# Ten token blocks with split products, loads moved behind the streamed sums, and plain last steps in a fused attention and rational expert kernel

## The chip, the cores and the metric

The kernel runs on one core of one Trainium2 chip. The metric is the device time of one execution in microseconds (us). The kernel before took 936.82 us (median of 2 runs, 936.0 to 937.63). The execution that the profiler recorded took 939.04 us; its span, from the first to the last instruction in the trace, is 937.3 us.

## The reference

Attention within chunks of 64 tokens (8 batches, 8 heads, 576 tokens, head size 64), and on its output a two-layer product with a rational function between:

```python
scores = scale * np.matmul(q_c, k_c.transpose(0, 1, 2, 4, 3))
attn = np.exp(scores - np.max(scores, axis=-1, keepdims=True))
attn = attn / (np.sum(attn, axis=-1, keepdims=True) + 1e-09)
x = np.matmul(attn, v_c)            # reshaped to 4608 tokens x 512
h = x @ w_in                        # 512 -> 2048
P = a[0] + a[1] * h + a[2] * h2 + a[3] * h3
Q = 1.0 + np.abs(b[0]) * np.abs(h) + np.abs(b[1]) * h2
g = P / (Q + 1e-06)
out = g @ w_out                     # 2048 -> 512
```

All inputs and the output are 32-bit floats.

## The kernel before

The 4608 tokens are cut into 18 blocks of 256 (`NB`), and the 2048 middle columns into 4 steps of 512 (`NST`), so there are 72 steps, numbered g = 4 x block + step. 32-bit values are kept as a high part and a low part, and a product of two such values is three matmuls: high by high, low by high, high by low.

**First layer.** A step's `ph` (512 middle columns by 256 tokens, a pair of PSUM banks) is 48 matmuls of 128x256 at L347 (`ff1`, in two halves that the order calls `F` and `Fb`). The first of them in a step multiplies `xhi` by `wi_hi`, the last multiplies `xhi` by `wi_lo`.

**The rational function.** ScalarE makes `U` = |h| and `C` from `ph`; VectorE and ScalarE work in turn until VectorE's third `C` instruction at L486 leaves g in `C` (entry `g` of the order).

**Second layer.** Up to block 5 a step is plain: ScalarE casts g to `ghi` (L496), GpSimd makes `glo` (L540), and TensorE does 48 matmuls at L423 into `po`. From block 6 on (`fast`) the product is a scheme of seven products of half the size each way: `graw` holds three quarters of g as they are, `shi`/`slo` four sums and differences of quarters (`B`, made on GpSimd at L505 to L537), and TensorE does 18 matmuls on `graw` (entries `Zr`, `Zr2`) and 24 on `shi` and `slo` (`Zs`, `Zl`), 42 in place of 48, at L594 into `acc` and `acd`. Four of the seven products need sums of quarters of w_out. They were made once, on GpSimd, during blocks 3 to 5 (`making`: up to six operations behind each `lS`; tiles `tt` and `hh`), and sent to scratch memory `t` (L568), 2 MB for each of the four steps. They don't all fit on the chip, so each step fetches its own from `t` again (`fetch`, L579): two transfers of 256 KB once `Zr2` has used the old ones (slot 0), one of 768 KB behind `Zs` and one behind `Zl` (slots 1 to 3). The sum products of the next step read them.

**Queue.** All transfers go through the queue of SyncE (SP): these fetches, `v` of the next block (L130, 512 KB, issued where the attention has used the old v, entry `A`), `qT` and `kT` of the next block (L754, 512 KB each, issued behind the scores, entry `S`), and the four stores of a block's output (L640, 128 KB each). An issue that has to wait, because its buffer is still read, holds up the ones behind it.

**Order.** In the steady state the string `STEADY` sets the order, entry by entry for a block; `_2` is a step, `-1` and `+1` the block before and after. Attention of the next block is spread over the entries in capitals with `+1`. Before it a hand-made list (`START`) covers 12 steps. TensorE runs a step's `ph` (48), then 42 products of the second layer of two steps back, and so on.

**End.** Behind the last `ph` come the second layer of the last two steps, then one copy (L624) and four additions (L630 to L636) that join `acc` and `acd` to the output tile `o`, and four stores.

Of the kernel before, what the change touches and what calls it, by code (L numbers as in the profile page):

```python
# [50 lines left out]
STEADY = (  # L51
# [6 lines left out]
)  # L58
# [6 lines left out]
def tile_chunked_attention_rational_moe(  # L65
# [28 lines left out]
    cst = cp.tile([P, 2], F32, tag="cst", name="cst")  # L94
    co = cp.tile([P, 32], F32, tag="co", name="co")
    a0, a1, a2, a3 = (ab[:, i:i + 1] for i in range(4))
# [3 lines left out]

    na0, na1, na2, na3, c0, kq, lsc, ebias, ib, b1m, nib = (co[:, i:i + 1] for i in range(11))
    TINY = 2.0 ** -60
# [228 lines left out]


    ch, gbuf, obuf, accs = {}, {}, {}, {}
# [94 lines left out]
    def newton_coefficients():  # L428
# [9 lines left out]
        ts(ebias, ebias, -KLN * math.log(2.0), None, ALU.add)  # L438

    def fast(g):  # L440
        return steps[g][0] >= FAST

# [88 lines left out]
    def new_ls(g):  # L531
# [3 lines left out]
        if fast(g):  # L535
            lo = gbuf[key][1] = p2.tile([P, 4, 2, 128], F32R, tag="glo", name=f"slo{g}")
            nc.gpsimd.tensor_sub(lo, sbuf[g], hi.bitcast(F32))  # L537
        else:
            lo = gbuf[key][1] = p2.tile([P, FPS, BT], F32R, tag="glo", name=f"glo{g}")
            nc.gpsimd.tensor_sub(lo, C, hi.bitcast(F32))  # L540

# [6 lines left out]
    def sums_of(s, tt, hh):  # L548
        def whole(dst, k, half):
            nc.gpsimd.tensor_add(dst, w_part(0, k, s, half).bitcast(F32), w_part(1, k, s, half).bitcast(F32))  # L550

        T = [tt[:, i] for i in range(4)]
        yield lambda: whole(T[1], 0, 0)
        yield lambda: whole(T[3], 0, 1)
        yield lambda: nc.gpsimd.tensor_sub(T[1], T[3], T[1])
        yield lambda: whole(T[2], 1, 1)
        yield lambda: nc.gpsimd.tensor_add(T[3], T[2], T[3])
        yield lambda: nc.gpsimd.tensor_add(T[2], T[2], T[1])
        yield lambda: whole(T[0], 1, 0)
        yield lambda: nc.gpsimd.tensor_sub(T[0], T[0], T[2])  # L560

        def low(i):
            nc.gpsimd.tensor_sub(tt[:, i], tt[:, i], hh[:, i].bitcast(F32))

        def send():
            scratch[s] = dr.tile([P, 2, 4, 512], F32, tag=f"t{s}", name=f"t{s}")
            nc.sync.dma_start(out=scratch[s][:, 0], in_=hh.bitcast(F32))
            nc.sync.dma_start(out=scratch[s][:, 1], in_=tt)  # L568

        yield lambda: nc.scalar.copy(hh[:, 1:4:2], tt[:, 1:4:2])  # L570
# [15 lines left out]

    def fast_product(n, s, name, j, stat, h, start, stop):
        where = FAST_B[name]
# [3 lines left out]
        else:  # L592
            mov = wo[:, h, FPS * where[3] + 2 * j, 256:512]
        nc.tensor.matmul(acc[n][pair][:, bank, col:col + 256], stat, mov, start=start, stop=stop)  # L594

# [3 lines left out]
    def fast_raw(g, half):  # L599
# [3 lines left out]
        for name in "124":  # L603
            for j in range(2):
                for h in ((0, 1) if half == 0 else (0,)):
                    stat = graw[g % 2][:, half, j, RAW[name]]
                    fast_product(n, s, name, j, stat, h, s == 0 and half == 0 and j == 0 and h == 0, False)

    def fast_sum(g, half):
        n, s = steps[g]  # L610
        for name in "5673":
            for j in range(2):
                for h in ((0, 1) if half == 0 else (0,)):
                    stat = gbuf[n, s][half][:, SUM[name], j]
                    fast_product(
                        n, s, name, j, stat, h, s == 0 and half == 0 and j == 0 and h == 0 and name == "7",
                        s == NST - 1 and half == 1 and j == 1,
                    )

    def fast_out(n, k):  # L620
# [14 lines left out]
        else:  # L635
            add(o[:, 1], one_[:, 1, 0:256], o[:, 1])  # L636
            for c in range(2):
                for u in range(UPB):
                    half = o[64 * u:64 * u + 64, 2 - 2 * c:4 - 2 * c].rearrange("p a b -> p (a b)")
                    (nc.scalar if n == NB - 1 and u else nc.sync).dma_start(out=rows_out(n)[c, u], in_=half)  # L640

# [87 lines left out]

    total = len(steps)  # L730
# [4 lines left out]
    making = [f for s in range(NST) for f in sums_of(s, tt, hh)]  # L735

# [12 lines left out]
    def next_scores(n):  # L749
        att_s(n, tag=other())  # L750
        if n + 1 < NB:
            for i, (src, key) in enumerate(((qT, "q"), (kT, "k"))):
                loaded[key, n + 1] = qk[:, i, :]
                nc.sync.dma_start(out=qk[:, i, :], in_=src[n + 1])  # L754

    def values(n):
        att_av(n, tag=other())
        load_v(n + 1)

# [6 lines left out]
    def step_op(op, g):  # L766
# [6 lines left out]
        elif op in chain:  # L773
            chain[op](g)
            if op == "lS":
                for _ in range(6):
                    if making:
                        making.pop(0)()
        elif not fast(g):
# [3 lines left out]
            elif op == "Zl":  # L783
                ff2(n, s, "po", 2)
                if n == FAST - 1:
                    for h in range(2):
                        fetch(0, slice(s, s + 1), h)
        elif op in ("Zr", "Zr2"):
            fast_raw(g, op == "Zr2")
            if op == "Zr2" and g + 1 < total:  # L790
                for h in range(2):
                    fetch((s + 1) % NST, slice(0, 1), h)
        else:
            fast_sum(g, op == "Zl")
            if g + 1 < total:
                fetch((s + 1) % NST, slice(1, 4), 1 if op == "Zs" else 0)

    items = [re.fullmatch(r"(\w+?)(?:_(\d))?([+-]\d+)?", item).groups() for item in STEADY.split()]
    for b in range(FIRST // NST, NB + 1):
        for op, stage, shift in items:  # L800
            n = b + int(shift or 0)
# [6 lines left out]
            elif op in ("P1", "o1", "o2", "o3", "o4"):  # L808
                if n >= FAST:
                    fast_out(n, ("P1", "o1", "o2", "o3", "o4").index(op))  # L810
                elif op == "P1" and n not in made["O"]:
                    store(n)
# [38 lines left out]
```

## Time and profile before

| | |
|---|---|
| time, median of 2 runs | 936.82 us |
| the profiled execution | 939.04 us, span 937.3 us |
| TensorE (PE) busy | 870.3 us, 93% of the span, 9096 matmuls |
| VectorE (DVE) busy | 749.6 us, 80% |
| ScalarE (ACT) busy | 562.9 us, 60% |
| GpSimd (POOL) busy | 506.2 us, 54% |
| DMA | 164.93 MB, mean 176 GB/s |
| mean granted TensorE clock | 0.978 |

The shares are means over the whole span: the first 280 us (loading, preparing the weights, the plain steps) look different from the 620 us behind them, in which blocks follow each other in about 48 us. The end, some 35 us without new `ph`, differs again. A view of waits says for how long an engine stood because something else was late, and what came last; a view of windows says the same by stretch. The chain of waits follows the end of the program backwards.

### The profile page before, as it was taken

What the parts mean: (1) busy time and instruction counts of PE and PEld (TensorE: products, weight loads), DVE (VectorE), ACT (ScalarE), POOL (GpSimd) and SP (SyncE); (2) the same over time, 40 slices, a digit from 0 to 9 for tenths busy, and PEclk for the clock granted to TensorE, in tenths of its full rate; (3) what the DMA queues carried; (4) which work ended last, traced back from release to release, by engine and by line L of the source; (5) the groups of instructions that cost most, each with busy time, mean ns of one, the idle gap of its engine ahead of it and who ended that gap; (6) DMA issues with size and microseconds to landing.
All of it is one profiled execution on the core that took longest, in us unless ns stands there. A gap on an engine that the chain in (4) does not pass through costs nothing.

```text
span 937.3 us, 20950 instructions
## 1 busy us (share of the span) xinstructions
PE 870.3 (93%) x9096; PEld 848.7 (91%) x9096; DVE 749.6 (80%) x673; ACT 562.9 (60%) x602; POOL 506.2 (54%) x318
## 2 busy tenths in 40 slices
PE   2799999989989999998999999999989999999985
PEld 1789999989989999898998999998989999999985
DVE  6899999867767687887778797878878889897771
ACT  4799966464455655555465656556556565666550
POOL 0114210236668635666567666675756767676672
PEclk9799999999999999999999999999999999999997
DMA  7455422102233243767576766667667777666673
GB/s 290 159 181 172 155 80 77 38 21 66 96 135 136 70 165 100 232 212 237 180 247 204 229 212 218 221 208 232 206 195 226 226 222 224 210 210 197 206 232 112
DMA packets 119099, 164.93 MB, mean 176 GB/s; under 512 B 5856, under 2 KB 104160, under 8 KB 115936
## 3 DMA queue, kind: packets, MB, share of 16 engines
q1 hardware_dynamic: 118848, 163.34, 54.4%
q8 instruction: 71, 1.16, 0.5%
q10 hardware_dynamic: 160, 0.26, 0.1%
q14 instruction: 20, 0.16, 0.1%
HBM read 145.76 MB, written 17.83 MB: 175 GB/s over the span
## 4 chain that ended last, share of the span: by engine, by line
PE 72%; DMA 13%; ACT 6%; DVE 5%; POOL 3%; issue 1%; DVEq 0%; SPq 0%; POOLq 0%; ACTq 0%
PE ph L347 34%; PE acc L594 12%; DMA wo<-t 11%; PE acd L594 10%; PE po L423 10%; PE psx L220 2%; DMA raw<-in_w_in 2%; PE pst L299 2%; PE pss L220 2%; ACT at L303 1%; DVE sm L256 1%; POOL glo L540 1%; DMA t<-tt 1%; POOL tt L550 1%; DVE e L262 1%
## 5 line engine op out<-in xcount | busy, mean ns | idle before, releaser
L347 PE MATMUL ph<-xhi,wi_hi 128*128 128x256 f32 x1152 | 326.1, 283 | 10.8 <-ACT at L303 6.4
L347 PE MATMUL ph<-xlo,wi_hi 128*128 128x256 f32 x1152 | 322.5, 280 | 0.1
L347 PE MATMUL ph<-xhi,wi_lo 128*128 128x256 f32 x1152 | 322.3, 280 | 0.0
L347 PEld LDWEIGHTS ph<-xhi,wi_hi 128*128 128x128 f32 x1152 | 217.8, 189 | 16.2 <-ACT at L303 8.6
L347 PEld LDWEIGHTS ph<-xlo,wi_hi 128*128 128x128 f32 x1152 | 217.8, 189 | 0.5 <-DVE xlo L330 0.4
L347 PEld LDWEIGHTS ph<-xhi,wi_lo 128*128 128x128 f32 x1152 | 217.9, 189 | 0.0
L537 POOL TENSOR_TENSOR slo<-B,shi 128x1024 fp32r<-128x1024 f32 x48 | 121.7, 2536 | 85.3 <-ACT shi L529 85.3
L478 DVE SCALAR_TENSOR_TENSOR U<-U,co,ph 128x1024 f32<-128x1024 f32 x60 | 75.7, 1261 | 58.2 <-ACT ph L474 58.2
L457 DVE SCALAR_TENSOR_TENSOR U<-U,co 128x1024 f32<-128x1024 f32 x60 | 98.9, 1649 | 26.4 <-ACT U L448 26.4
L448 ACT ACTIVATE U<-ph 128x1024 f32<-128x1024 f32 x60 | 61.5, 1025 | 91.4 <-PE ph L347 91.4
L505 POOL TENSOR_TENSOR graw<-C,graw 128x768 fp32r<-128x768 f32 x48 | 98.7, 2055 | 31.0 <-ACT graw L500 24.6
L513 POOL TENSOR_TENSOR B<-C 128x512 f32<-128x512 f32 x48 | 75.1, 1564 | 70.7 <-DVE C L486 70.7
L470 ACT ACTIVATE B<-U,cst,co 128x1024 f32<-128x1024 f32 x60 | 74.8, 1246 | 54.7 <-DVE U L457 54.7
L461 DVE TENSOR_TENSOR C<-C,ph 128x1024 f32<-128x1024 f32 x60 | 72.8, 1214 | 33.6 <-ACT U L448 33.6
L423 PE MATMUL po<-wo,ghi 128*128 128x256 f32 (+2 forms) x768 | 93.5, 278 | 0.0
L453 ACT ACTIVATE C<-ph,co 128x1024 f32<-128x1024 f32 x60 | 72.2, 1204 | 31.2 <-PE ph L347 28.0
L423 PEld LDWEIGHTS po<-wo,ghi 128*128 128x128 f32 x768 | 90.6, 188 | 0.0
L594 PE MATMUL acc<-wo,graw 128*128 128x256 f32 x576 | 84.6, 281 | 1.5 <-POOL graw L505 1.5
L474 ACT ACTIVATE ph<-B,co 128x1024 f32<-128x1024 f32 x60 | 67.2, 1120 | 29.1 <-DVE C L465 26.8
L594 PE MATMUL acd<-wo,shi 128*128 128x256 f32 x384 | 64.5, 292 | 21.6 <-DMA wo<-t 19.9
L486 DVE SCALAR_TENSOR_TENSOR C<-C,co,ph 128x1024 f32<-128x1024 f32 x60 | 76.9, 1281 | 2.1
L465 DVE SCALAR_TENSOR_TENSOR C<-C,co,ph 128x1024 f32<-128x1024 f32 x60 | 76.6, 1276 | 1.1
(107 smaller groups left out, 1630.8 us busy)
## 6 DMA issues: line engine op xcount, KB each, us to landing
wo<-t SPq DMA_DIRECT2D x94, 768.0 KB, 6.5
wo<-t SPq DMA_DIRECT2D x102, 256.0 KB, 3.5
v<-in_vP SPq DMA_DIRECT2D x18, 512.0 KB, 4.8
out<-o SPq DMA_DIRECT2D x70, 128.0 KB, 2.6
raw<-in_w_in SPq DMA_DIRECT2D x8, 1024.0 KB, 4.8
raw<-in_w_out SPq DMA_DIRECT2D x8, 1024.0 KB, 4.8
qk<-in_qT SPq DMA_DIRECT2D x16, 512.0 KB, 3.6
qk<-in_kT SPq DMA_DIRECT2D x16, 512.0 KB, 5.0
```

Of the source, the lines that this page charges most:

```text
L347: nc.tensor.matmul(ph[:, fi, :], w[:, cc, f], x[:, cc, :], start=(k == 0), stop=(k == len(mm) - 1))
L423: nc.tensor.matmul(accs[n][i][:, cols], g[:, fi, i * 128:(i + 1) * 128], w[:, FPS * s + fi, cols], start=start, stop=stop,)
L457: nc.vector.scalar_tensor_tensor(U, U, c0, U, ALU.add, ALU.mult)
L461: nc.vector.tensor_mul(C, C, h)
L465: nc.vector.scalar_tensor_tensor(C, C, na1, h, ALU.add, ALU.mult)
L470: nc.scalar.activation(ch[key][2], ch[key][1], AF.Ln, bias=cst[:, 0:1], scale=lsc)
L478: nc.vector.scalar_tensor_tensor(V, V, kq, h, ALU.add, ALU.mult)
L486: nc.vector.scalar_tensor_tensor(C, C, na0, h, ALU.add, ALU.mult)
L505: nc.gpsimd.tensor_sub(lo, quads(ch[steps[g]][3])[:, :, 1:4, :], hi.bitcast(F32))
L513: nc.gpsimd.tensor_sub(S[:, 0:2], q[:, 0:1].to_broadcast([P, 2, 2, 128]), q[:, 1:3])
L537: nc.gpsimd.tensor_sub(lo, sbuf[g], hi.bitcast(F32))
L594: nc.tensor.matmul(acc[n][pair][:, bank, col:col + 256], stat, mov, start=start, stop=stop)
```

## The change

Six things change together.

1. **Parts.** In blocks 7 to 16 certain matmuls are written as two, each for a part of the 256 columns of the moving operand, with the same stationary operand. F is the first `ph` product of a step, f the last, r the first product on `graw`, l the last on `slo`. The cuts are 152/104 (MOST), 128/128 (EVEN) and 208/48 (SOME). Twelve products by four steps are cut, 48 more matmuls in all.
2. **Loads.** `qk`, `v` and the output stores no longer go out at their own entries. They are put on a list, and behind each step's last fetch two entries of the list are sent: `qT`/`kT` in four pieces of 256 columns (128 KB each), `v` in two halves of 256 KB, the stores in pairs. Two entries are 512 KB.
3. **Last steps.** `fast` leaves out g = 70 and 71. They are plain steps again, 96 matmuls in place of 84, into a bank pair of their own (`pe`); `glo` is made on VectorE. The quarters of w_out that the fetches overwrite are kept in scratch `b` and loaded again as `b12` (1 MB, at the start of the last block). The joining of `acc` and `acd` is done before, and two additions into `oe` and stores of 256 KB (halves on two queues) end the program.
4. **Making.** `making` is cut into groups: four operations, four operations, then copies, low parts and the send, so that twelve `lS` entries carry it and no longer ten.
5. **Order.** `STEADY` has another order of entries for VectorE, ScalarE and GpSimd. TensorE's order of entries is the same.
6. **Places.** The tile of constants `co` moves to another pool, and `graw` starts 384 bytes into its buffer.

```diff
+    PARTS = {
+        7: {"F": MOST}, 8: {"r": MOST}, 9: {"F": MOST, "r": MOST}, 10: {"F": EVEN}, 11: {"r": EVEN},
+        12: {"f": MOST}, 13: {"l": MOST}, 14: {"f": MOST, "l": MOST}, 15: {"F": SOME}, 16: {"r": SOME},
+    }
...
             for k, (w, x, cc) in enumerate(mm):
-                nc.tensor.matmul(ph[:, fi, :], w[:, cc, f], x[:, cc, :], start=(k == 0), stop=(k == len(mm) - 1))
+                at_ = "F" if fi == 0 and k == 0 else "f" if fi == FPS - 1 and k == len(mm) - 1 else ""
+                cuts = parts_of(n, at_)
+                for i, (a_, b_) in enumerate(cuts):
+                    nc.tensor.matmul(
+                        ph[:, fi, a_:b_], w[:, cc, f], x[:, cc, a_:b_], start=(k == 0 and i == 0),
+                        stop=(k == len(mm) - 1 and i == len(cuts) - 1),
+                    )
...
     def fast(g):
-        return steps[g][0] >= FAST
+        return NST * FAST <= g < total - 2
...
-            graw[g % 2] = p2.tile([P, 2, 2, 3, 128], F32R, tag="raw", name=f"graw{g % 2}", bufs=3)
+            t = p2.tile([P, 96 + 1536], F32R, tag="raw", name=f"graw{g % 2}", bufs=3)
+            graw[g % 2] = t[:, 96:].rearrange("p (h j q t) -> p h j q t", h=2, j=2, q=3)
...
+    def tail_load():
+        b12 = p2.tile([P, 2, 2, 2, 256], F32R, tag="raw", name="b12", bufs=3)
+        tail["b12"] = b12
+        for k in range(2):
+            nc.sync.dma_start(out=b12.bitcast(F32)[:, k], in_=scratch["b", 2 + k])
...
-                nc.sync.dma_start(out=qk[:, i, :], in_=src[n + 1])
+            for c in range(4):
+                def send(c=c):
+                    cols = slice(256 * c, 256 * c + 256)
+                    for i, src in enumerate((qT, kT)):
+                        nc.sync.dma_start(out=qk[:, i, cols], in_=src[n + 1][:, cols])
+
+                later.append(send)
...
-                for _ in range(6):
-                    if making:
-                        making.pop(0)()
+                while making:
+                    f = making.pop(0)
+                    if f is None:
+                        break
+                    f()
...
+        elif g == total - 2:
+            if op in ("Zr", "Zl"):
+                tail_next(int(op == "Zl"))
+        elif g == total - 1:
+            if op == "Zl":
+                tail_last()
...
             fast_sum(g, op == "Zl")
-            if g + 1 < total:
+            if fast(g + 1):
                 fetch((s + 1) % NST, slice(1, 4), 1 if op == "Zs" else 0)
+            if op == "Zl":
+                later_loads()
+
+    def later_loads():
+        for f in later[:2]:
+            f()
+        del later[:2]
...
+        if b == NB - 1:
+            tail_load()
```

The queue of SP, one block in the steady state, before. `t` is a step's scratch, `wo` the place that the products read.

```order
L640 DMA out<-o_6278 64x512 x4
L579 DMA wo<-t_2883 128x2x256 x2
L130 DMA v_6407<-in_vP 128x1024
L579 DMA wo<-t_2883 128x6x256 x2
L754 DMA qk<-in_qT 128x1024
L754 DMA qk<-in_kT 128x1024
L579 DMA wo<-t_3179 128x2x256 x2
L579 DMA wo<-t_3179 128x6x256 x2
L579 DMA wo<-t_3631 128x2x256 x2
L579 DMA wo<-t_3631 128x6x256 x2
```

The same stretch of SP's queue in the changed kernel:

```order
L721 DMA out<-o_6933 64x512 x4
L604 DMA wo<-t_3471 128x2x256 x2
L604 DMA wo<-t_3471 128x6x256 x2
L852 DMA v_7060<-in_vP 128x512 x2
L604 DMA wo<-t_3931 128x2x256 x2
L604 DMA wo<-t_3931 128x6x256 x2
L842 DMA qk<-in_qT 128x256
L842 DMA qk<-in_kT 128x256
```

Before, one step's fetches have 1 MB of `qk` ahead of them and the slots 1 to 3 of another have `v`; now each step's fetches come first, and 512 KB of other transfers follow them.

GpSimd while the sums of w_out are made, before:

```order
L550 TENSOR_TENSOR tt<-wo 128x512 x2
L555 TENSOR_TENSOR tt<-tt 128x512
L550 TENSOR_TENSOR tt<-wo 128x512
L557 TENSOR_TENSOR tt<-tt 128x512
L558 TENSOR_TENSOR tt<-tt 128x512
L540 TENSOR_TENSOR glo_2454<-C_2200,ghi_2399 128x1024
L550 TENSOR_TENSOR tt<-wo 128x512
L560 TENSOR_TENSOR tt<-tt 128x512
L563 TENSOR_TENSOR tt<-tt,hh 128x512 x2
L540 TENSOR_TENSOR glo_2584<-C_2338,ghi_2535 128x1024
L563 TENSOR_TENSOR tt<-tt,hh 128x512 x2
L550 TENSOR_TENSOR tt<-wo 128x512 x2
```

and in the changed kernel:

```order
L557 TENSOR_TENSOR glo_2452<-C_2197,ghi_2377 128x1024
L576 TENSOR_TENSOR tt<-tt 128x512
L577 TENSOR_TENSOR tt<-tt 128x512
L567 TENSOR_TENSOR tt<-wo 128x512
L579 TENSOR_TENSOR tt<-tt 128x512
L557 TENSOR_TENSOR glo_2611<-C_2336,ghi_2494 128x1024
L583 TENSOR_TENSOR tt<-tt,hh 128x512 x4
L557 TENSOR_TENSOR glo_2744<-C_2530,ghi_2661 128x1024
L567 TENSOR_TENSOR tt<-wo 128x512 x2
```

Before, the first operations of the next step's sums (L550, which overwrite `tt`) stand directly behind the last operations of this step's, with only the transfer that empties `tt` between; now a `glo` stands there.

The end of VectorE's program, before (the last rational function, then the joining of `acc` and `acd`):

```order
L461 TENSOR_TENSOR C_10437<-C_10437,ph_3_10366 128x1024
...
L478 SCALAR_TENSOR_TENSOR U_10439<-U_10439,co,ph_3_10366 128x1024
L482 SCALAR_TENSOR_TENSOR ph_3_10366<-U_10439,ph_3_10366 128x1024
L486 SCALAR_TENSOR_TENSOR C_10437<-C_10437,co,ph_3_10366 128x1024
L630 TENSOR_TENSOR o_10590<-acc_10305,o_10590 128x2x256
L632 TENSOR_TENSOR o_10590<-acd_10306,o_10590 128x2x256
L634 TENSOR_TENSOR o_10590<-acd_10306,o_10590 128x512
L636 TENSOR_TENSOR o_10590<-acc_10305,o_10590 128x256
```

and in the changed kernel:

```order
L494 SCALAR_TENSOR_TENSOR U_10579<-U_10579,co,ph_3_10509 128x1024
L557 TENSOR_TENSOR glo_10622<-C_10460,ghi_10581 128x1024
L498 SCALAR_TENSOR_TENSOR ph_3_10509<-U_10579,ph_3_10509 128x1024
L502 SCALAR_TENSOR_TENSOR C_10584<-C_10584,co,ph_3_10509 128x1024
L557 TENSOR_TENSOR glo_10677<-C_10584,ghi_10659 128x1024
L708 TENSOR_TENSOR o_10679<-acc_10443,o_10679 128x2x256
...
L714 TENSOR_TENSOR o_10679<-acc_10443,o_10679 128x256
L692 TENSOR_TENSOR oe_10709<-pe,o_10679 128x512
L692 TENSOR_TENSOR oe_10737<-pe,o_10679 128x512
```

The two `glo` of the last steps have come to VectorE, and the four additions stand ahead of the last two, which alone read the last products (`pe`).

## Rows read from the trace of the kernel before

**Rows 1.** The profile's page, section 2: in 40 equal slices of the span the granted clock of TensorE in tenths of full speed, and the busy share of the DMA engines in tenths.

```profile
PEclk9799999999999999999999999999999999999997
DMA  7455422102233243767576766667667777666673
```

**Rows 2.** What TensorE waited for over the whole span: the waiting operation and its line, what came last, then us in total, times, and the longest.

```profile
PE acd L594 <- DMA wo<-t: 20.5, 12, 3.7
...
PE ph L347 <- ACT at L303: 6.4, 11, 4.7
```

**Rows 3.** The same view for 367 to 902 us alone, in which the seven-product steps follow each other.

```profile
PE acd L594 <- DMA wo<-t: 14.6, 9, 3.0
```

**Rows 4.** Busy time by windows, each one block of the steady state, and the sum over nine such windows: the window, its length, busy us of the engines (and instructions), granted clock, DMA share, GB/s.

```profile
433.23:484.31 51.08, 47.97 (x497) 47.08 (x497) 40.01 (x36) 28.16 (x28) 31.53 (x21) 0.97 0.66 207
484.31:532.27 47.96, 45.72 (x497) 44.86 (x497) 39.65 (x36) 28.15 (x28) 31.83 (x21) 1.00 0.70 222
...
726.57:773.49 46.92, 46.38 (x497) 45.32 (x497) 39.61 (x36) 28.18 (x28) 32.17 (x21) 1.00 0.72 224
...
sum 435.45, PE 417.58 PEld 409.48 DVE 360.48 ACT 253.41 POOL 287.01; mean PE 46.40 PEld 45.50 DVE 40.05 ACT 28.16 POOL 31.89
```

**Rows 5.** The chain of waits from 484 to 535 us: start, us, what.

```profile
484.18 10.07 DMA wo<-t
...
495.08 0.45 PE acc L594 x4
...
497.34 5.44 PE ph L347 x48
502.79 0.94 PE acc L594 x8
...
504.67 0.70 PE acd L594 x6
...
508.72 5.92 PE ph L347 x48
```

**Rows 6.** The timeline of SP's queue from 460 to 505 us: start, us until the end of the piece, line, transfer, number.

```profile
480.81 0.35 SPq L754 DMA_DIRECT2D qk<-in_qT  x1
...
481.74 23.56 SPq L579 DMA_DIRECT2D wo<-t  x9
```

**Rows 7.** The fetches issued between 484.1 and 485 us: time from issue to landing.

```profile
DMA to landing us min/median/max: 10.1/10.1/10.1
```

**Rows 8.** The two fetches issued between 496 and 498 us, in a step without other transfers: when, and time from issue to landing.

```profile
L579 SPq DMA_DIRECT2D wo<-t x2: 359/360/360, 496.0 to 497.1; - x2
...
DMA to landing us min/median/max: 4.7/5.3/5.8
```

**Rows 9.** The page's section 6, issues of transfers: number, KB each, median us from issue to landing.

```profile
wo<-t SPq DMA_DIRECT2D x94, 768.0 KB, 6.5
...
out<-o SPq DMA_DIRECT2D x70, 128.0 KB, 2.6
...
qk<-in_kT SPq DMA_DIRECT2D x16, 512.0 KB, 5.0
```

**Rows 10.** Busy time by short windows: two right behind the two longest waits of the steady state, and one without a wait before it (columns as in rows 4).

```profile
444.00:448.60 4.60, 4.41 (x24) 4.44 (x25) 4.50 (x7) 2.51 (x3) 3.44 (x4) 0.63 0.26 71
686.30:690.80 4.50, 4.35 (x24) 4.38 (x25) 4.40 (x6) 2.42 (x3) 3.82 (x4) 0.62 0.37 107
590.00:592.90 2.90, 2.72 (x23) 2.75 (x24) 2.86 (x3) 1.65 (x2) 2.82 (x3) 1.00 0.51 165
```

**Rows 11.** The chain of waits while the sums of w_out are made, 225 to 275 us.

```profile
229.25 2.38 POOL glo L540
...
235.14 6.76 DMA t<-tt
...
260.87 7.36 PE ph L347 x48
```

**Rows 12.** The timeline of VectorE at the end of the program: start, us, line, operation.

```profile
912.81 1.28 DVE L486 SCALAR_TENSOR_TENSOR C<-C,co,ph 128x1024 f32<-128x1024 f32 x1
...
932.00 0.69 DVE L634 TENSOR_TENSOR o<-acd,o 128x512 f32<-128x512 f32 x1
932.60 0.41 DVE L636 TENSOR_TENSOR o<-acc,o 128x256 f32<-128x256 f32 x1
```

**Rows 13.** The chain of waits at the end of the program.

```profile
902.98 0.94 PE acc L594 x8
...
907.72 6.53 DMA wo<-t
...
919.45 5.93 DMA wo<-t
```

**Rows 14.** Busy time by windows at the end of the program (columns as in rows 4).

```profile
907.93:930.11 22.18, 14.72 (x84) 13.76 (x83) 4.76 (x4) 4.12 (x4) 10.66 (x7) 0.77 0.54 175
```

**Rows 15.** The casts to `ghi` on ScalarE, a group by line: number, busy us, mean ns of one, idle before.

```profile
L496 ACT CAST ghi<-C 128x1024 fp32r<-128x1024 f32 x12 | 12.5, 1044 | 2.9 <-DVE C L486 2.9
```

**Rows 16.** Products of the plain second layer (L423), shapes apart: number, busy us, mean ns of one, idle before.

```profile
L423 PE MATMUL po<-wo,ghi 128*128 128x304 f32 x32 | 9.5, 297 | 0.0
L423 PE MATMUL po<-wo,ghi 128*128 128x208 f32 x32 | 8.3, 259 | 0.0
```

More of the change, by code (lines that the diff above doesn't have):

```diff
@@ L568, in send @@
             nc.sync.dma_start(out=scratch[s][:, 1], in_=tt)
+            if s >= 2:
+                scratch["b", s] = dr.tile([P, 2, 2, 256], F32, tag=f"b{s}", name=f"b{s}")
+                rows = slice(FPS * s, FPS * s + 3, 2)
+                for h in range(2):
+                    nc.sync.dma_start(out=scratch["b", s][:, h], in_=wo.bitcast(F32)[:, h, rows, 256:512])
         yield lambda: nc.scalar.copy(hh[:, 1:4:2], tt[:, 1:4:2])
@@ L593, in fast_product @@
             mov = wo[:, h, FPS * where[3] + 2 * j, 256:512]
-        nc.tensor.matmul(acc[n][pair][:, bank, col:col + 256], stat, mov, start=start, stop=stop)
+        cuts = parts_of(n, place_)
+        for i, (a_, b_) in enumerate(cuts):
+            nc.tensor.matmul(
+                acc[n][pair][:, bank, col + a_:col + b_], stat, mov[:, a_:b_],
+                start=start and i == 0, stop=stop and i == len(cuts) - 1,
+            )
     RAW = {"1": 0, "2": 2, "4": 1}
@@ L606, in fast_raw @@
                     stat = graw[g % 2][:, half, j, RAW[name]]
-                    fast_product(n, s, name, j, stat, h, s == 0 and half == 0 and j == 0 and h == 0, False)
+                    first = s == 0 and half == 0 and j == 0 and h == 0
+                    at_ = "r" if half == 0 and j == 0 and h == 0 and name == "1" else ""
+                    fast_product(n, s, name, j, stat, h, first, False, at_)
     def fast_sum(g, half):
@@ L636, in fast_out @@
             add(o[:, 1], one_[:, 1, 0:256], o[:, 1])
+            if n == NB - 1:
+                return
             for c in range(2):
-                for u in range(UPB):
-                    half = o[64 * u:64 * u + 64, 2 - 2 * c:4 - 2 * c].rearrange("p a b -> p (a b)")
-                    (nc.scalar if n == NB - 1 and u else nc.sync).dma_start(out=rows_out(n)[c, u], in_=half)
+                def send(c=c):
+                    for u in range(UPB):
+                        half = o[64 * u:64 * u + 64, 2 - 2 * c:4 - 2 * c].rearrange("p a b -> p (a b)")
+                        nc.sync.dma_start(out=rows_out(n)[c, u], in_=half)
+                later.insert(c, send)
     def rows_out(n):
@@ L727, in tile_chunked_attention_rational_moe @@
     run(START, "F")
-    total = len(steps)
+    co = p2.tile([P, 32], F32, tag="co", name="co", bufs=1)
+    na0, na1, na2, na3, c0, kq, lsc, ebias, ib, b1m, nib = (co[:, i:i + 1] for i in range(11))
     newton_coefficients()
@@ L734, in tile_chunked_attention_rational_moe @@
     qk = p2.tile([P, 2, W], F32, tag="raw", name="qk", bufs=3)
-    making = [f for s in range(NST) for f in sums_of(s, tt, hh)]
+    making = [f for s in range(NST) for f in sums_of(s, tt, hh)][1:]
     made = {name: {int(args.split(".")[0]) for name_, args, _ in START_ITEMS if name_ == name} for name in "SEZTKAXYNO"}
@@ L753, in next_scores, with send @@
                 loaded[key, n + 1] = qk[:, i, :]
-                nc.sync.dma_start(out=qk[:, i, :], in_=src[n + 1])
+            for c in range(4):
+                def send(c=c):
+                    cols = slice(256 * c, 256 * c + 256)
+                    for i, src in enumerate((qT, kT)):
+                        nc.sync.dma_start(out=qk[:, i, cols], in_=src[n + 1][:, cols])
+                later.append(send)
     def values(n):
         att_av(n, tag=other())
-        load_v(n + 1)
+        if n + 1 < NB:
+            v = loaded["v", n + 1] = p2.tile([P, W], F32, tag="vt", name=f"v{n + 1}", bufs=1)
+            for c in range(2):
+                cols = slice(512 * c, 512 * c + 512)
+                later.append(lambda cols=cols: nc.sync.dma_start(out=v[:, cols], in_=vP[n + 1][:, cols]))
     attention = {
@@ L787, in step_op @@
                         fetch(0, slice(s, s + 1), h)
+                later_loads()
         elif op in ("Zr", "Zr2"):
             fast_raw(g, op == "Zr2")
-            if op == "Zr2" and g + 1 < total:
+            if op == "Zr2" and fast(g + 1):
                 for h in range(2):
@@ L808, in tile_chunked_attention_rational_moe @@
             elif op in ("P1", "o1", "o2", "o3", "o4"):
[L809 removed]
+                if NB - 1 > n >= FAST:
                     fast_out(n, ("P1", "o1", "o2", "o3", "o4").index(op))
[L811 removed]
+                elif op == "P1" and n < FAST and n not in made["O"]:
                     store(n)
```

55 lines of the change are left out of this document (50 added, 5 removed), and 12 rows, old and new, of the table STEADY.

## The prediction

> **What bounds the kernel now.** I read the clock and the DMA shares by slice first, then TensorE's waits, then one block at a time, and the end apart. TensorE runs at nearly full clock in every slice, and the DMA engines have room as a mean [rows 1]; what the change can win is the time in which TensorE stands or runs slowly. A block takes 46.92 to 51.08 us, of which TensorE is busy 45.72 to 47.97, while VectorE has 39 to 41, GpSimd 32 and ScalarE 28 [rows 4]. So TensorE sets the pace, and what is left over is mostly one wait: the sum products on `acd` wait for the fetched weight sums, 14.6 us in nine waits between 367 and 902 us [rows 3], 20.5 us with the three at the end [rows 2].
>
> Why the fetch is late shows once per block. At 480.81 the loads of `qk`, 1 MB, go on the queue, and the fetches follow at 481.74 [rows 6]. The fetch issued at 484.18 lands 10.07 us later [rows 5, 7], where the fetches of a step without other transfers land in 4.7 to 5.8 us [rows 8]. In that quiet step the last fetch, issued at 497.1, is there at 502.9. The first sum product comes after two of the raw ones that start at 504.67 [rows 5], so at about 504.9. A fetch has 2.0 us to spare when nothing is ahead of it, and is late when `qk` or `v` is.
>
> **The change part by part.**
>
> *Loads behind the fetches.* Each step's fetches now come first, so the nine waits go: -14.6 us. What follows is 512 KB a step, in the same total as before. The next fetch is issued when slot 0 comes free, at the end of the raw products, some 8 us after the last one of the step before. A block moves its bytes at 222 GB/s with a DMA share of 0.70 [rows 4], so about 317 GB/s at full share; a step's 2.5 MB are 8.3 us of its 11.9 (a quarter of 47.5). The queue drains, with little room where attention makes a step's spacing uneven. I leave 1.5 us of waits: **-13.1 us**. Bounds: -14.6, and 0 if the wait only changes its cause.
>
> *Clock.* Behind the two longest waits TensorE ran at a granted clock of 0.63 and 0.62, near the 1.2 GHz level for most of it: 24 products in 4.41 and 4.35 us, where 23 take 2.72 at 1.00 [rows 10], that is 184 and 181 ns each against 118. 24 x 66 ns and 24 x 63 ns are 1.6 and 1.5 us. Both waits go: **-3.1 us** (bounds -3.1 and 0).
>
> *Making of the sums.* Here TensorE stood 4.7 us for `at` [rows 2] and then took 7.36 us for a run of 48 [rows 11] that takes 5.44 to 5.92 elsewhere [rows 5]; I set 5.66 as the middle, so 1.7 us. The chain leads back through a 6.76 us transfer that empties `tt` [rows 11], for which GpSimd waited with the next `glo` behind it. With a `glo` between, that transfer lies beside other work, and the groups of four keep GpSimd's share of a step short. **-6.4 us** (bounds -6.4, and 0 if `tt` is still late, since ScalarE's `ghi` and `at` hang on GpSimd in the same order).
>
> *End.* TensorE stands for the last fetches in two pieces of 6.53 and 5.93 us of chain [rows 13], and the stretch from 907.93 to 930.11 holds 14.72 us of products, at a clock of 0.77 [rows 14]. Now no fetch is needed there. The last g is ready at 912.81 + 1.28 = 914.1 [rows 12]; that chain of VectorE and ScalarE hangs on the last `ph` and stays, the added `glo` fitting its idle time. The cast to `ghi` takes 1.04 us [rows 15], to 915.1. In the meantime TensorE has 42 products of step 69 and 48 of step 70, at 0.94 / 8 = 118 ns [rows 13] 10.6 us from 903.0, so it stands about 1.5 us and should keep its clock. The last 48 products take 5.7 us, to 920.8; VectorE's `glo` (1.2 us) and the four earlier additions lie beside them. One addition of 0.69 us [rows 12] gives 921.5. From the end of the last addition before (932.60 + 0.41 [rows 12]) to the end of the span (937.3) the stores took 4.3 us; the two halves of 256 KB on two queues are the same bytes, so 925.8. **-11.5 us**. Bounds: 2.7 us worse if the 48 run at the 175 ns of the old stretch (14.72 / 84 [rows 14]), and 1 us better if the stores land sooner.
>
> *Split products.* 48 more matmuls, all on TensorE's path. No row has one narrower than 208 columns. 96 columns fewer shorten a product from 297 to 259 ns [rows 16], 0.40 ns a column, so 256 columns are 102 of a product's 118 ns and 16 ns are paid per product: 48 x 16 ns = 0.8 us. The other bound is a full product for each, 48 x 118 ns = 5.7 us, if the weights loaded again (all 128 columns in either part) set the pace. I take 40 ns, nearer the first since a part of 208 columns still shortens: **+1.9 us**. The Trainium skill, "TensorE: Matmul & The Clock Gate", section "LDWEIGHTS (loading the stationary operand)", gives a load as its columns over 1.2 in ns, 107 for 128; by that both parts would take at least 107 ns and 48 splits some 4.6 us (an estimate from that page), and the sum would be 2.7 us longer. Section "Back-to-back issue gap" of the same page has a pair of load and product of 128 columns at 81 ns, by which it would be about 2.1 us; no row here decides between them.
>
> *Reload of `b12` and places.* 1 MB once, like `qk` of old, ahead of fetches in the last block, and one more send of 512 KB in two of the four makings: **+1.5 us** (bounds 0, and 4 for one fetch late by 10.07 - 5.8 us [rows 5, 8]).
>
> *Spacing of products.* Products stand either 113 or 118 ns apart: a run of `ph` takes 5.44 us (113 ns x 48), and the four sum products 0.45; eight raw ones take 0.94, always the slow spacing [rows 5]. Moving `graw` and `co` may deal these anew. I take half of the raw ones to the fast one, 9 x 46 steps x 5 ns: **-2.0 us**. Bounds: -12 if the slow runs of `ph`, most of them, go fast too (some 48 x 5 ns = 0.24 us in 50 steps), and +5 if the fast ones go slow.
>
> *Order on the other engines.* VectorE at 40 of 48 us has 15% to spare [rows 4], and the same instructions; 0, bounds -1 and +3.
>
> Sum: -13.1 - 3.1 - 6.4 - 11.5 + 1.9 + 1.5 - 2.0 = -32.7 us. The profiled execution took 939.04, which is 2.2 above the median of the runs, 936.8. 939.0 - 32.7 = 906.3, and on the median **904**.
>
> **The rivals.**
>
> *Waits persist (912 to 925).* 512 KB behind every fetch, in more pieces, keep the queue from draining before the next fetch, or the making or the clock at the end stay as they were. For it: the margin of 2.0 us. Against: every block has room at a share of 0.70 [rows 4]. Half of the loads' gain (8 us) and the making (6.4) lost, or one of them: 12%.
>
> *All runs go to the fast spacing (885 to 895).* 904 - 10. For it: the raw ones are all slow and the run of 5.44 shows that the fast spacing holds through 48 products. Against: nothing before shows that places decide it. 13%.
>
> *Little is won (918 to 955).* The sums would have to be late for a reason other than `qk` and `v`; the landing of 10.07 against 5.8 us [rows 5, 8] speaks against it. Splits at their full price (+3.8), no gain in the making (+6.4) and half the loads' gain gone together give 919. 8%.
>
> *Slower (956 and above): the queue never drains.* The 48 steps of blocks 6 to 17 each have 512 KB in pieces of 128 or 256 KB, and if these go slowly, every step's fetch is late by L and the wait comes 48 times in place of nine. To be 2% slower the change has to lose 32.7 + 18.7 = 51.4 us, so it decides from L = 1.1 us a step; with the 2.0 us to spare, the queue would need 3.1 us more a step than now. A 128 KB store lands in 2.6 us and a 512 KB load in 5.0 [rows 9]: four pieces one after the other would be 10.4, or 5.4 us more, and L would be 3.4 us, the kernel 904 + 163 = 1067. Against it: the pieces need not wait for each other, and two fetches of 768 KB overlap already [rows 8]. 4%. The Trainium skill, "DMA: Bandwidth & Descriptors", section "Measured (HBM→SBUF, 128 partitions, SWDGE, issued from GpSimd)", asks for batches of 1 MiB or more and shows 138 GB/s at 64 KB against 341 at 1 MB, which speaks for this rival; the rows here show no such transfer on its own.
>
> **Chances.** My forecast (895 to 912) has 63%, the others as given. About 2% is what a measurement of this kernel can tell from no change: below 918.1 faster, above 955.6 slower. Faster 0.86 (forecast, fast spacing, and nearly all of the persisting waits), same 0.10, slower 0.04. The range 887 to 918 takes in the fast spacing but its last part, the forecast and the persisting waits up to the bound.
>
> **What would show it.** In the changed profile `acd` waits for `wo<-t` should be under 2 us in the steady state and gone at the end; blocks 47 us long; `v` and `qk` behind the fetches on the queue; the run of 48 after the making near 5.66 with no wait for `at`; the last `pe` product some 18 us after the last `ph`; blocks 9 and 14, with 8 more matmuls each, less than a microsecond longer than block 6. Wrong it would be if acd waits move from one step to every step, if the raw products' spacing falls to 113 (then I am too high), or if a split costs 100 ns and more.

## The result and the profile after

The changed kernel takes **902.33 us** (median of 2 runs, 902.31 to 902.34) against 936.82 before: a ratio of 0.9638, 95% interval 0.9562 to 0.9713. The profiled execution took 902.34 us, its span is 900.2 us, against 939.04 and 937.3 before.

The page: busy time of the engines, and by 40 slices the granted clock and the DMA share.

```profile
PE 860.3 (96%) x9156; PEld 840.7 (93%) x9156; DVE 764.2 (85%) x677; ACT 556.3 (62%) x600; POOL 478.3 (53%) x308
...
PEclk9799999999999999999999999999999999999999
DMA  7444341202224255685868676867777777675860
```

TensorE has 60 matmuls more and 10 us less of busy time; one slice of lower clock at the end, and most of its standing, are gone [rows 1]. What is left of its waits (operation, what came last, us, times, longest):

```profile
PE pe L668 <- ACT ghi L512: 1.5, 1, 1.5
PE ph L358 <- ACT at L301: 1.3, 8, 0.2
PE pe L668 <- DVE oe L692: 1.1, 1, 1.1
...
PE acd L621 <- DMA wo<-t: 0.8, 2, 0.5
```

The waits for fetches have gone from 20.5 us to 0.8, that for `at` from 6.4 to 1.3 [rows 2]; two new ones of 1.5 and 1.1 us stand at the end. Two blocks of the steady state by windows (columns as in [rows 4]) and the sum over nine:

```profile
420.50:466.00 45.50, 45.32 (x499) 44.60 (x498) 40.80 (x36) 27.75 (x29) 30.58 (x20) 1.00 0.73 230
466.00:512.90 46.90, 46.60 (x505) 45.73 (x504) 41.55 (x36) 27.71 (x29) 30.35 (x20) 1.00 0.73 227
...
sum 415.25, PE 413.28 PEld 406.67 DVE 371.15 ACT 249.48 POOL 273.89; mean PE 45.92 PEld 45.19 DVE 41.24 ACT 27.72 POOL 30.43
```

Nine blocks take 415.25 us where nine took 435.45 [rows 4], at a clock of 1.00. SP's queue in such a block (start, us until the end of the piece, transfer), and the page's landings (number, KB, median us):

```profile
432.87 3.21 SPq L604 DMA_DIRECT2D wo<-t  x4
436.12 0.54 SPq L842 DMA_DIRECT2D qk<-in_qT  x1
...
437.45 0.74 SPq L842 DMA_DIRECT2D qk<-in_qT  x1
```

```profile
wo<-t SPq DMA_DIRECT2D x90, 768.0 KB, 6.7
...
qk<-in_qT SPq DMA_DIRECT2D x48, 128.0 KB, 6.7
```

The fetches are issued first and land in 6.7 us as a median, near the 6.5 of before [rows 9]. The pieces of `qk`, which nobody waits for, now take 6.7 us for 128 KB.

**Where the time went**, between the same events of the two traces (starts of a block's scores on TensorE): up to 229 us +0.6; the next block, in which the sums of w_out are made, 56.2 to 49.5, -6.7; two blocks after it -0.6; nine steady blocks 435.1 to 415.2, -19.8; from there to the end 121.5 to 110.9, -10.6. In all -37.1 us of span.

The chain where the sums are made, and at the end of the program (start, us, what):

```profile
233.25 5.72 PE ph L358 x48
...
244.59 5.48 PE ph L358 x48
```

```profile
870.16 5.47 PE ph L358 x48
...
883.87 1.14 DVE glo L557
...
886.17 1.29 DVE C L502
...
887.57 1.05 ACT ghi L512
...
892.16 0.69 DVE oe L692
...
892.90 3.11 PE pe L668 x24
896.03 0.69 DVE oe L692
```

The run of 48 at 233.25 takes 5.72 us where 7.36 stood [rows 11], with no wait for `at` ahead of it. At the end nothing of `wo<-t` is left in the chain [rows 13]. The last `ph` ends at 875.63, the last g at 887.46, the cast at 888.62; the last 24 products start at 892.90, and the program ends 24.6 us after the last `ph`, where it was 34.3.

Runs of `ph` in the chain (49 matmuls where one is split; MOST at 379.01, none at 425.34, EVEN at 517.83):

```profile
379.01 5.56 PE ph L358 x49
...
425.34 5.46 PE ph L358 x48
...
517.83 5.57 PE ph L358 x49
```

With the last `ph` product split (609.74) and with SOME (782.50), and then the first raw products of two steps, eight without a split and nine with one (MOST):

```profile
609.74 5.50 PE ph L358 x49
...
782.50 5.56 PE ph L358 x49
```

```profile
441.37 0.91 PE acc L621 x8
...
452.92 1.02 PE acc L621 x9
```

These are runs at the fast spacing (other runs, with or without a split, take longer, up to 6.0 us). At that spacing a run without a split takes 5.46 us, with one 5.50 to 5.57; the raw ones take 0.91 and 1.02. Where the run with a split last product is only 0.04 longer, the rest of the price falls behind it: the first raw spacing there is 182 or 183 ns in place of 113 or 114. The products one by one, at the cut EVEN and at the cut SOME (start, us, operation; x2 are the two parts):

```profile
517.67 0.33 PE L358 MATMUL ph<-xhi,wi_hi 128*128 128x128 f32 x2
517.84 0.33 PE L358 MATMUL ph<-xlo,wi_hi 128*128 128x256 f32 x1
518.01 0.28 PE L358 MATMUL ph<-xhi,wi_lo 128*128 128x256 f32 x1
```

```profile
782.33 0.30 PE L358 MATMUL ph<-xhi,wi_hi 128*128 128x208 f32 x2
782.47 0.36 PE L358 MATMUL ph<-xlo,wi_hi 128*128 128x256 f32 x1
782.67 0.28 PE L358 MATMUL ph<-xhi,wi_lo 128*128 128x256 f32 x1
```

The two parts and the product behind them take 0.34 us from start to start (517.67 to 518.01, 782.33 to 782.67), and as much at the cut MOST. Two products without a split take 0.23 to 0.24 us. So each split costs 0.10 to 0.12 us, for every one of the three cuts.

### The profile page after: what moved, and what is told of

The parts are those of the page before. It is cut to its first block, busy times and chain, and to the rows that moved or that the text cites. A ratio compares the mean times of both kernels' runs of the same rounds, so it can differ in the third digit from the quotient of the medians.

```text
span 900.2 us, 21188 instructions
## 1 busy us (share of the span) xinstructions
PE 860.3 (96%) x9156; PEld 840.7 (93%) x9156; DVE 764.2 (85%) x677; ACT 556.3 (62%) x600; POOL 478.3 (53%) x308
## 4 chain that ended last, share of the span: by engine, by line
PE 85%; DVE 7%; ACT 5%; DMA 2%; issue 1%; SPq 0%; DVEq 0%; ACTq 0%
PE ph L358 43%; PE acc L621 13%; PE po L437 12%; PE acd L621 10%; PE psx L218 2%; PE pss L218 2%; PE pst L297 2%; ACT at L301 1%; DVE sm L254 1%; DMA wo<-t 1%; DVE e L260 1%; DMA Bqk<-in_kT 1%; PE pl L197 1%; DVE xlo L328 1%; ACT e L273 1%
## 5 line engine op out<-in xcount | busy, mean ns | idle before, releaser
L358 PE MATMUL ph<-xhi,wi_hi 128*128 128x256 f32 (+2 forms) x1168 | 324.2, 280 | 5.9 <-DVE e L260 2.7
L358 PE MATMUL ph<-xhi,wi_lo 128*128 128x256 f32 (+2 forms) x1160 | 321.1, 278 | 0.0
L554 POOL TENSOR_TENSOR slo<-B,shi 128x1024 fp32r<-128x1024 f32 x46 | 110.5, 2403 | 73.2 <-ACT shi L546 73.2
L473 DVE SCALAR_TENSOR_TENSOR U<-U,co 128x1024 f32<-128x1024 f32 x60 | 94.4, 1573 | 26.1 <-ACT U L464 26.0
L522 POOL TENSOR_TENSOR graw<-C,graw 128x768 fp32r<-128x768 f32 x46 | 92.2, 2004 | 42.4 <-ACT graw L517 42.3
L621 PE MATMUL acc<-wo,graw 128*128 128x256 f32 (+4 forms) x568 | 81.8, 280 | 0.0
L498 DVE SCALAR_TENSOR_TENSOR ph<-U,ph 128x1024 f32<-128x1024 f32 x60 | 73.4, 1224 | 1.2
```

The source lines that it names most:

```text
L358: nc.tensor.matmul(ph[:, fi, a_:b_], w[:, cc, f], x[:, cc, a_:b_], start=(k == 0 and i == 0), stop=(k == len(mm) - 1 and i == len(cuts) - 1),)
L473: nc.vector.scalar_tensor_tensor(U, U, c0, U, ALU.add, ALU.mult)
L498: nc.vector.scalar_tensor_tensor(h, V, 2.0, h, ALU.subtract, ALU.mult)
L522: nc.gpsimd.tensor_sub(lo, quads(ch[steps[g]][3])[:, :, 1:4, :], hi.bitcast(F32))
L621: nc.tensor.matmul(acc[n][pair][:, bank, col + a_:col + b_], stat, mov[:, a_:b_], start=start and i == 0, stop=stop and i == len(cuts) - 1,)
```

## The experiments

Times are medians; runs of the kernel before on the same chips gave 936 to 940 us.

**Splits taken out.** Only `PARTS` is emptied.

```diff
-    PARTS = {
-        7: {"F": MOST}, 8: {"r": MOST}, 9: {"F": MOST, "r": MOST}, 10: {"F": EVEN}, 11: {"r": EVEN},
-        12: {"f": MOST}, 13: {"l": MOST}, 14: {"f": MOST, "l": MOST}, 15: {"F": SOME}, 16: {"r": SOME},
-    }
+    PARTS = {}
```

> The changed kernel with none of the 48 splits. By the price the prediction took (40 ns each) it is 1.9 us faster than the changed kernel's 902.3: 900.4. Rival: each split costs nearly a whole product (100 to 118 ns): 4.8 to 5.7 us faster, 896.6 to 897.5; in the changed profile a run of ph with a split first product takes 5.56 us where one without takes 5.45, which speaks for it. Second rival: the splits are what set the runs of ph to the fast spacing; without them they go back to 5.66 us from 5.45 in some 40 steps, and the kernel is some 5 us slower, 907.

Measured: 897.87 us, ratio to before 0.9582 (0.9531 to 0.9634); span 897.7. That lies at the rival of a whole product each, 4.5 us below the changed kernel by the medians, 2.5 by the spans (2.9 and 3.9 in a second measurement, the last run below). It is the fastest kernel here. The runs of `ph` did not go back to 5.66: 1231 of 1728 `ph` products in nine blocks stand at 112 to 115 ns, so the fast spacing does not need the splits (the last run below qualifies the number).

**More splits.** F, f, r and l in two halves in all seven-product steps.

```diff
+    PARTS = {n: {"F": EVEN, "f": EVEN, "r": EVEN, "l": EVEN} for n in range(6, NB)}
```

> The changed kernel with F, f, r and l all cut in two halves of 128 columns in every seven-product step: 188 splits in place of 48, 140 more. If a split costs about a whole product, as the runs of the changed kernel show for all three cuts (0.10 to 0.12 us), it takes 902.3 + 140 x 0.11 = 917.7 us. Rival: 40 ns each, as the prediction took: 907.9. Second rival: two halves of the same weights overlap once nothing else is late: 903 to 905.

Measured: 919.99 us (0.9791, 0.9750 to 0.9832); span 913.5. One block by windows, of this kernel and of the one without splits:

```profile
658.70:705.80 47.10, 46.99 (x514) 46.44 (x514) 41.59 (x36) 27.78 (x29) 30.17 (x20) 1.00 0.70 225
```

```profile
647.90:693.20 45.30, 45.14 (x497) 44.58 (x496) 40.65 (x36) 27.59 (x29) 30.63 (x20) 1.00 0.72 233
```

47.10 us with 16 splits against 45.30 with none: 0.11 us for each. Against the changed kernel the 140 more cost 13.3 us by the spans, 0.095 each, and 17.7 by the medians, 0.126. The price of 40 ns is refuted from both sides. (These are net prices: the spacing of the whole products differs between the kernels too.)

**Loads at their old entries.** The pieces stay, but are sent at once where the old kernel sent its loads.

```diff
-    later = []
+    class AtOnce(list):
+        def append(self, f):
+            f()
...
+        def insert(self, c, f):
+            f()
...
+    later = AtOnce()
```

> The changed kernel, with qk, v and the stores sent at their old entries (qk ahead of a step's fetches), in the same small pieces. If the place in the queue is what made the fetches late, acd waits for wo<-t again once or so per block, 10 to 14 us, with up to 3 us of half clock behind them: 912 to 919. Rival: the pieces, or the other order of entries, took the waits away: 902 to 905.

Measured: 934.76 us (0.9978, 0.9939 to 1.0017), 32 us above the changed kernel, twice what was expected: all that the change wins is gone. TensorE's wait between 372 and 820 us, and SP's queue around one issue of `qk`:

```profile
PE acd L621 <- DMA wo<-t: 22.9, 9, 3.5
```

```profile
470.24 0.34 SPq L849 DMA_DIRECT2D qk<-in_qT  x1
...
473.49 0.42 SPq L849 DMA_DIRECT2D qk<-in_kT  x1
474.01 1.99 SPq L604 DMA_DIRECT2D wo<-t  x4
```

The nine waits are back, one a block, and they are longer than before (22.9 against 14.6 us [rows 3]). Eight issues of `qk` hold the fetch up from 470.24 to 474.01, 3.8 us, where two took 0.9 [rows 6]: small pieces cost issue time on SP, which ahead of a fetch is late time. The other part of the 32 us, which I had put at 3 at most, is the clock: in four of the nine blocks the granted clock is 0.94 to 0.97, and TensorE is busy 8 us longer in the nine. So the place in the queue carries the steady state's gain, and the small pieces need that place.

**Only the loads, on the kernel before.** Whole transfers of 512 KB and stores in pairs, behind each step's fetches.

```diff
-                nc.sync.dma_start(out=qk[:, i, :], in_=src[n + 1])
+                later.append(lambda i=i, src=src: nc.sync.dma_start(out=qk[:, i, :], in_=src[n + 1]))
+                later.append(lambda: None)
...
+            if op == "Zl":
+                later_loads()
```

> The kernel before, with only the loads moved: qT, kT and v as whole transfers of 512 KB and the stores in pairs, two entries of the list behind each step's fetches. Theory: this alone takes away the nine waits of the steady state (14.6 us) and the half clock behind two of them (3.1 us): 936.8 - 16 to 18 = 919 to 921, and the wait for at and the end stay. Rival: with the old order of entries the fetches are late in other steps, and it gains half or less: 928 to 937.

Measured: 920.85 us (0.9824, 0.9766 to 0.9883), at the upper end of what was expected. The wait between 370 and 860 us:

```profile
PE acd L601 <- DMA wo<-t: 2.1, 2, 1.2
```

The same nine blocks take 416.4 us, all but a microsecond of what the whole change gives them. The move of the loads is worth 15 to 16 us by itself (936.0 in the same chip's runs of the kernel before, 936.8 in the first). The whole change gives these blocks more and takes it back: without splits they take 411.7 and 412.7 us (first and last run here). Against 411.7 the products at the fast spacing are 793 fewer in the kernel before with its loads moved; at 5 ns each that is 4.0 us, most of the difference. The 44 splits in these blocks cost about as much.

**Whole loads in the changed kernel.** Without splits, qT, kT and v as one transfer of 512 KB each.

```diff
-            for c in range(4):
-                def send(c=c):
-                    cols = slice(256 * c, 256 * c + 256)
...
+            for i, src in enumerate((qT, kT)):
+                later.append(lambda i=i, src=src: nc.sync.dma_start(out=qk[:, i, :], in_=src[n + 1]))
+                later.append(lambda: None)
```

> The changed kernel without splits, with qT, kT and v each as one transfer of 512 KB behind a step's fetches, in place of pieces of 128 and 256 KB. If the place in the queue is all that counts, it takes the same 897 to 899 and waits for wo<-t stay near 2 us. Rival (pieces keep the queue from draining): it becomes faster, 895 to 896. Second rival (a whole transfer holds up the next fetch): waits grow by 3 us and more, 901 to 906.

Measured: 902.86 us (0.9612, 0.9577 to 0.9647); span 898.6, against 897.7 and 896.3 of the two runs with pieces. Waits for `wo<-t` were 4.1 us, against 2.2 and 0.4. By its median it lies where the second rival stands, but the waits grew by 2 to 4 us and the spans by 1 to 2. Pieces are no worse behind the fetches and perhaps better by a few us; a larger transfer won nothing.

**Making by sixes again.**

```diff
-                while making:
-                    f = making.pop(0)
-                    if f is None:
-                        break
-                    f()
+                for _ in range(6):
+                    if making:
+                        making.pop(0)()
```

> The changed kernel, with the making of the weight sums in groups of six operations again. If the grouping is what removed the wait for at, the wait of 4 to 5 us and a slow run of ph behind it come back: 907 to 909. Rival: the new order of entries removed it: 902 to 903.

Measured: 907.34 us (0.9672, 0.9618 to 0.9726), as expected of the grouping. The chain:

```profile
231.55 7.31 DMA t<-tt
...
257.79 0.92 ACT at L301
...
258.76 7.43 PE ph L358 x48
```

The transfer that empties `tt` is in the chain again, `at` is late (3.6 us) and the run behind it takes 7.43 us.

**Last steps by seven products.** With their fetches, without `b12`.

```diff
-        return NST * FAST <= g < total - 2
+        return NST * FAST <= g < total
```

> The changed kernel, with the last two steps by the seven products again, with their fetches, and no b12. If the plain last steps are worth what the prediction says (11.5 us less 1.5 for the reload), it takes 912 to 914. Rival: with the loads behind the fetches the last fetches come in time anyway, and the plain steps gain only the shorter way to the last g: 904 to 907.

Measured: 910.5 us (0.9714, 0.9663 to 0.9766), 8.2 above the changed kernel, between the two expectations; it is the price of the end and of the reload of `b12` together. The fetches stand in the chain at the end:

```profile
877.64 7.21 DMA wo<-t
...
889.25 6.38 DMA wo<-t
```

7.21 and 6.38 us, no shorter than before [rows 13]: having the other loads behind them did not help the last fetches.

**Places.** Without splits: `co` back in its old pool, which puts all tiles behind it 128 bytes higher; and, in another kernel, `graw` back at the start of its buffer.

```diff
-    co = p2.tile([P, 32], F32, tag="co", name="co", bufs=1)
+    co = cp.tile([P, 32], F32, tag="co", name="co")
```

> The changed kernel without splits, with the tile of constants co back in its old pool, so that every tile behind it lies 128 bytes higher, as before. Theory: the places of the tiles set the spacing of ph; most runs of ph go back from 5.45 to 5.66 us, in half or more of some 50 steps: 5 to 10 us slower than without splits (897.9), 903 to 908, and in the trace more runs of 5.66 than of 5.45. Rival: the places of ph's operands do nothing, the new order of entries on the other engines set the spacing: 897 to 899.

```diff
-            t = p2.tile([P, 96 + 1536], F32R, tag="raw", name=f"graw{g % 2}", bufs=3)
-            graw[g % 2] = t[:, 96:].rearrange("p (h j q t) -> p h j q t", h=2, j=2, q=3)
+            graw[g % 2] = p2.tile([P, 2, 2, 3, 128], F32R, tag="raw", name=f"graw{g % 2}", bufs=3)
```

> The changed kernel without splits, with graw at the start of its buffer again. Theory: its place sets the spacing of the 18 raw products, which go back from 113 to 118 ns in some 46 steps, as the prediction's term of 2.0 us says it: some 2 to 4 us slower than 897.9, 900 to 902. Rival: the spacing of the raw products comes from the run of ph ahead of them: 897 to 899, and raw products as without this edit.

Measured: 902.39 us (0.9612, 0.9581 to 0.9642) and 900.65 (0.9589, 0.9547 to 0.9630). With `co` back, 724 of 1728 `ph` products stand at 112 to 115 ns; with `graw` back, 42 of 648 raw ones, and 1346 of `ph`. By time they stand 3.0 to 4.5 and 1.2 to 2.8 us above the two measurements of the kernel without splits (897.87 and 899.44), too near for the time alone to decide.

**`co` moved in the kernel before.**

> The kernel before, with only the tile of constants moved to the other pool, so that every tile behind it lies 128 bytes lower. Theory: the places set the spacing of ph, so that most runs take 5.45 us in place of 5.66, in some 50 steps; the waits for fetches take part of it back: 3 to 8 us faster than before, 929 to 934. Rival: places matter only with the new order: 936 to 938.

Measured: 939.18 us (1.0023, 0.9986 to 1.0060), no gain; the fast `ph` products are 759 of 1728, against 520 before.

**The old order of entries**, without splits.

> The changed kernel without splits, with the order of entries (STEADY) of the kernel before. The prediction set the order on the other engines at 0 (-1 to +3): 897 to 901, waits as without this edit. Rival: the old order makes sums or casts late for TensorE, or the wait for at comes back although the making is in the new groups: 903 and more.

Measured: 902.87 us (0.963, 0.957 to 0.969), span 902.7. The nine blocks take 412.7 us, against 411.7 and 412.7 without this edit; of the 5.0 us by which the span is longer than 897.7, 3.6 lie ahead of 234 us, in the beginning of the program. No effect on the steady state. Whether the beginning owes its 3.6 us to the order is open: one wait in it, 1.9 us at 114 us, stands with 1.5 us in the run with `graw` back too, which has the new order.

**The kernel without splits again.**

> The changed kernel without splits once more, to see how much of the differences in spacing between the runs so far is chance. Theory (the places decide): in nine blocks some 1230 of 1728 ph products stand at 113 ns again, within 50, raw ones some 420 of 648, and the time is 897 to 899. Rival (each run deals the spacing anew): counts as far off as the 1061 and 1001 of the runs with whole loads and with the old order, and times that spread by 3 us and more.

Measured: 899.44 us (0.9580, 0.9553 to 0.9607), span 896.3; 925 fast `ph` products where the same kernel had 1231, and 323 raw ones where it had 416. Its wait between 370 and 850 us:

```profile
PE acd L618 <- DMA wo<-t: 0.4, 1, 0.4
```

So a part of the spacing differs from one execution to the next. Counts between 925 and 1346 for `ph` say nothing by themselves. The 42 of 648 with `graw` back lie far outside that, and the kernels with `graw` at its old place all have few fast raw products (10, 14, 20 and 42). But the place alone does not decide: the kernel with 188 splits has `graw` at the new one and only 37 of 684. The splits may bear on `ph` too: of the changed kernels, those with splits have 1245 to 1629 there at 112 to 115 ns, those without 724 to 1346. For `co` the evidence points the same way (724 and 520 with the old place, 759 and up with the new) but 759 against 724 is close, closer than two executions of one kernel, and what sets the spacing of `ph` stays open.

## Why the prediction was right, and where not

The time was 902.3 where 904 was forecast. The loads, the clock and the making came out about as worked; the splits, the spacing and the end were mis-sized, and that the total is closer than its parts is luck. Between the two profiled executions, on which the terms were worked, -32.7 us was forecast and -36.7 came; the 2.2 us taken off for the median make the forecast look closer. Two of the signs that I had named for being wrong came true: a split costs 100 ns and more, and many raw products went to 113 ns.

- **Loads behind the fetches (-13.1, clock -3.1).** Right. 0.8 us of waits are left, less than the 1.5 that I kept, and the clock is 1.00 in all nine blocks. The kernel before with this part alone won 15 to 16 us.
- **Making (-6.4).** Right: -6.7 between the same events, 5.0 when only the grouping is undone.
- **End (-11.5).** Too large by about 2: 24.6 us from the last `ph` to the end, in place of 34.3, so -9.7, and 8.2 in the experiment. Two steps failed. "The added `glo` fitting its idle time" did not hold: it stands in the chain at 883.87 for 1.14 us, and the cast came 13.0 us after the last `ph` in place of 12.1. And the first 24 of the last products are followed by a wait of 1.1 us for VectorE's addition on the first half of `pe`, which itself stood behind the four additions on `o`; I had put those beside the products. So the last `pe` product came 20.4 us after the last `ph`, where some 18 were forecast. The clock stayed at full level there, and the 1.5 us of standing before the cast came out as worked, though the products and the cast on either side of it both came about 1 us later.
- **Splits (+1.9).** Mis-sized. "I take 40 ns" is the step that failed: 0.10 to 0.12 us each, so 48 cost about 5.3 us. I reasoned from 0.40 ns a column between 208 and 304 columns; in place of that, two parts cost as much time as two whole products, however the columns are cut. The upper bound of 5.7 us was near. That the weights loaded again are the reason was its condition, and no run shows it apart from the split. Taking all 48 out won only 2.5 to 4.5 us; the spacing differed too. The Trainium skill, "TensorE: Matmul & The Clock Gate", section "LDWEIGHTS (loading the stationary operand)", gives 107 ns for a load of 128 columns. The trace comes near it: three loads and products in 0.34 us are about 114 ns each. By the same page's 81 ns for a pair of load and product at 128 columns, section "Back-to-back issue gap", a split in halves would cost about 0.05 us (2 x 81 less 113 ns, an estimate from that page). The halves here cost twice that.
- **Spacing (-2.0).** Mis-sized, and by the wrong products. In nine blocks the `ph` products at 112 to 115 ns went from 520 of 1728 to 1444 (of 1752), the raw ones from 10 of 648 to 355 of 660, while those on sums went the other way, from 532 of 864 to 101 of 872. At 5 ns each that is 4.6 + 1.7 - 2.2 = 4.1 us; what is left of the 19.8 us of the nine blocks after waits of all kinds (17.6 to 1.5 us, so 16.1), clock (3.1) and 44 splits (-4.8) is 5.4. The errors of splits and spacing, +3.4 and -2 to -3.4, nearly cancel.
- **Reload of `b12` (+1.5).** Little of it shows: one wait of 0.5 us for a fetch in the last block. No run tries it apart.
- **Order (0).** Right for the steady state by the run with the old order; for the beginning of the program, where that run is 3.6 us longer, it stays open.
- **Rivals.** The queue that never drains did not come: 0.68 to 0.73 of DMA share in the nine blocks and 0.3 us of waits for fetches. The rule of the Trainium skill that speaks for it ("DMA: Bandwidth & Descriptors", section "Measured (HBM→SBUF, 128 partitions, SWDGE, issued from GpSimd)": large batches) did not decide here, since whole loads were no faster; where the pieces did harm, with the loads early, the trace shows the issue time on SP. The time that I gave for little being won, 919, was added up wrongly: 904 + 3.8 + 6.4 and half of 13.1 are 921.

## What to carry to other kernels

When a stream of fetches has little room, look at what stands ahead of it in the queue, and send what nobody awaits soon behind it: here that alone was worth 15 to 16 us, and eight small issues ahead of a fetch took 3.8 us on the queue where two large ones took 0.9. Here a product cut in two cost as much as two products, so cut none without a need. At the end of a program, an engine that the last dependent steps share (VectorE here) can take back a part of what a removed fetch gives: about 2 of the 11.5 us forecast here.

## What the runs showed that I had not expected

A product split at 48, 104 or 128 of 256 columns costs 0.10 to 0.12 us, whatever the cut. The spacing of the products, 113 or 118 ns, changes from one execution of the same kernel to the next (1231 and 925 of 1728), and moving `graw` by 384 bytes took the raw products at 113 ns from 42 to more than 300 of 648, but not in the kernel where every first raw product is split (37 of 684). What decides between the two spacings stays open.
